# A diffusion block with adaptive layer norm: fewer and larger early loads, and the first rows of scale behind the transposes

## The chip, the cores and the metric

The kernel runs on one core of a Trainium2 chip. The core has a matrix engine (TensorE, PE in the profile, with PEld for its weight loads), a vector engine (VectorE, DVE), an activation engine (ScalarE, ACT), a general engine (GpSimd, POOL) and SyncE (SP), whose queue issues nearly all loads and stores. Sixteen DMA engines move the data between the chip's main memory (HBM) and the on-chip memory (SBUF); TensorE writes to accumulators in PSUM.

The metric is the time of one execution on the device, in microseconds (us); lower is better.

## The reference

B = 2 sequences of N = 256 tokens, width D = 1152, all tensors in bfloat16. Scale, shift and gate come from the vector c; the tokens are normalised, modulated, and go through one attention of a single head.

```python
mod = (_silu(c) @ w_mod).reshape(B, 6, 1, D)
shift_a, scale_a, gate_a, shift_m, scale_m, gate_m = [mod[:, i] for i in range(6)]
h = _layernorm(x, axis=-1) * (1 + scale_a) + shift_a
qkv = h @ wqkv
q, k, v = (qkv[..., :D].copy(), qkv[..., D:2 * D].copy(), qkv[..., 2 * D:].copy())
p = _softmax(jnp.einsum('bqd,bkd->bqk', q, k) * D ** (-0.5), axis=-1)
a = jnp.einsum('bqk,bkd->bqd', p, v) @ wo
return x + gate_a * a
```

Only the first three of the six parts of w_mod are used: shift (0), scale (1) and gate (2).

## The kernel before

**Tiles.** The 512 tokens are four tiles of 128 (t = 0 and 1 are sequence 0, t = 2 and 3 sequence 1). The width of 1152 is KT = 9 blocks of 128. The blocks fall into three parts of KA = 3: columns 0 to CA = 384, CA to CM = 768, and CM to D. w_mod is laid out with nine rows kk for each partition (line 49), so that a sum over c's width is a sum over the nine rows, and the kernel speaks of "rows" of scale and shift in this sense. K's weights (wK) have nine rows k, one for each block of the width of h.

**Loads.** Line 142 on defines `load_x` (a token tile, 288 KB), `load_mod` (some rows and columns of one part of w_mod) and `load_k` (rows and columns of K's weights); lines 151 to 174 issue them on SP's queue in this order: x tiles 1, 0 and 3; the first part of scale, as five loads of two rows (the last of one); K's row 0 in two pieces (3 blocks, then the 5 that are left of the first WE = 1024 columns), row 1, x tile 2, K's row 2; scale's second part in three loads of three rows; K's rows 3 to 5; scale's third part in three loads; K's rows 6 to 8; shift (wH) in five loads of two rows, the last of one; what is left of K's rows 0 to 2. The loads of Q's and V's weights, of the gate and of wo follow on the same queue. Eight completion semaphores are used in turn, so that a load on this queue is issued when the eighth load before it (the one of c counted) has landed; before, the first load that waits so is the fifth one of scale. c is loaded by ScalarE's queue.

**Opening on TensorE.** Twelve products of a constant tile (`fillers(12)`, line 185) come first, then two products that put the 1 of (1 + scale) into the accumulators psSA and psS0. `scale_A(kk)` (line 298) adds one row of the first part of scale: three products of 54 columns, into psS0 for block 0 and psSA for blocks 1 and 2. `turned` transposes the nine blocks of a centred token tile (xc) into two banks of PSUM (tp1a and tp1b, tp0a and tp0b), and `from_psum` copies them out to xnT, three blocks on VectorE and six on ScalarE. Lines 382 to 396 set the order: scale rows 0 and 1; tile 1's transposes and copies; rows 2 and 3; tile 0's transposes and copies; rows 4 to 8.

**After it.** `scaled(0, tok(0), psS0[:, 0:1])` on VectorE multiplies block 0 of sequence 0 with its finished scale, straight from psS0, and writes hTs; `k_part` (line 335) then starts to sum K in six accumulators (accs) and `early_half` a part of the next two blocks (psE). Tiles 3 and 2 follow in the same way. The second part of scale is summed in psM (rows 0 to 5, other work, then rows 6 to 8), the third in psL (all nine rows in one go), and the shift in psH by `shift_rows` (36 products, line 321). Then come Q, the scores, V, the attention and the output, all on TensorE, while VectorE works on the gate.

**Order.** The order of instructions on each engine is that of the program: each engine's calls are recorded by a helper (`_Rec`, line 78, which is why the profile gives L78 for nearly all of them) and chained by `pin` at the end. So the groups are told apart by the tiles that they write and read.

Of the kernel before, what the change touches and what calls it, by code (L numbers as in the profile page):

```python
# [16 lines left out]
def kernel(  # L17
# [11 lines left out]
    B, N, D = x.shape  # L29
    T = B * N  # L30
    KT = D // P
# [9 lines left out]
    WE = (NACC + NEARLY) * P  # L41
# [97 lines left out]
    wS = wmpool.tile([P, KT, D], BF16, tag="wS")  # L139
    wH = wmpool.tile([P, KT, D], BF16, tag="wH")  # L140

    def load_x(t):
        spq.dma_start(out=x_sb[:, t, :], in_=x_f[t * P : (t + 1) * P, :])

    def load_mod(tile_, which, k0, k1, c0, c1):
        spq.dma_start(out=tile_[:, k0:k1, c0:c1], in_=wmod_v[:, k0:k1, which, c0:c1])

    def load_k(k0, k1, c0=0, c1=D):
        spq.dma_start(out=wK[:, k0:k1, c0:c1], in_=wqkv_v[:, k0:k1, D + c0 : D + c1])

    PAIRS = ((0, 2), (2, 4), (4, 6), (6, 8), (8, 9))
    CA = KA * P
    load_x(1)
    load_x(0)
    load_x(3)
    for k0, k1 in PAIRS:
        load_mod(wS, 1, k0, k1, 0, CA)
    load_k(0, 1, 0, CA)
    load_k(0, 1, CA, WE)
    load_k(1, 2, 0, WE)  # L160
    load_x(2)
    load_k(2, 3, 0, WE)
    CM = KM * P
    for k0 in range(0, KT, 3):
        load_mod(wS, 1, k0, k0 + 3, CA, CM)
    for k in range(KA, KM):
        load_k(k, k + 1)
    for k0 in range(0, KT, 3):
        load_mod(wS, 1, k0, k0 + 3, CM, D)
    for k in range(KM, KT):  # L170
        load_k(k, k + 1)
    for k0, k1 in PAIRS:
        load_mod(wH, 0, k0, k1, 0, D)
    load_k(0, KA, WE, D)

# [28 lines left out]
    def sc_rhs(kk):  # L204
        return scT_rep[:, kk].rearrange("p r b -> p (r b)")
# [37 lines left out]
    def turned(tp, cols):  # L243
        for j, (t, k) in enumerate(cols):
            ten.transpose(tp[:, j, :], xc[:, t, k * P : (k + 1) * P], ident)

    def tiles_of(t, k0, k1):
        return [(t, k) for k in range(k0, k1)]

    def from_psum(eng, t, k0, k1, tp, j0=0):  # L250
        dst, srct = xnT[:, k0:k1, t * P : (t + 1) * P], tp[:, j0 : j0 + k1 - k0, :]
        if eng is vec:
            vec.tensor_copy(out=dst, in_=srct)
        else:
            sca.copy(out=dst, in_=srct)
# [42 lines left out]
    def scale_A(kk):  # L298
        for j in range(KA):
            ten.matmul(  # L300
                psS0 if j == 0 else psSA[:, j - 1, :], lhsT=wS[:, kk, j * P : (j + 1) * P], rhs=sc_rhs(kk),
                start=False, stop=(kk == KT - 1), skip_group_check=True,
            )
# [75 lines left out]
    def bank(name="tp", n=KT - KA, pool=psum, tag="mm"):  # L379
        return pool.tile([P, n, P], BF16, tag=tag, name=name)  # L380

    tp1a, tp1b, tp0a, tp0b = bank(n=KA), bank(), bank(n=KA), bank()
    for kk in range(2):
        scale_A(kk)
    turned(tp1a, tiles_of(1, 0, KA))
    turned(tp1b, tiles_of(1, KA, KT))
    from_psum(vec, 1, 0, KA, tp1a)
    from_psum(sca, 1, KA, KT, tp1b)
    for kk in range(2, 4):
        scale_A(kk)  # L390
    turned(tp0a, tiles_of(0, 0, KA))
    turned(tp0b, tiles_of(0, KA, KT))
    from_psum(vec, 0, 0, KA, tp0a)
    from_psum(sca, 0, KA, KT, tp0b)
    for kk in range(4, KT):
        scale_A(kk)
    act_var(0)

# [333 lines left out]
```

## Time and profile before

| what | value |
|---|---|
| time, median of 3 runs (lowest to highest) | 96.02 us (95.85 to 96.29) |
| the profiled execution: its own time, its span | 95.77 us, 94.0 us |
| TensorE's matmuls, of the whole span | 89.7 us (95%), 677 instructions |
| 12 fillers (junk_ps) | 1.11 to 6.41 us |
| first product on K (acc) | 8.86 us |
| loads moved by DMA engines, over the span | 21.31 MB, mean 227 GB/s |

The profile is of one execution. Its span runs from the first instruction of the program to the last; the execution's own time is 1.77 us longer. Times inside the profile are counted from the start of the span. A weight load (PEld) lies beside matmuls (PE) and precedes the product that uses it. Matmuls are pipelined: the times of single ones overlap, and the chain of waits gives each the time that it adds. "Landing" is when the last of a load's parts has told its semaphore, and the DMA view gives the time from issue to landing.

### The profile page before, as it was taken

What the parts mean: (1) busy time and instruction counts of PE and PEld (TensorE: products, weight loads), DVE (VectorE), ACT (ScalarE), POOL (GpSimd) and SP (SyncE); (2) the same over time, 40 slices, a digit from 0 to 9 for tenths busy, and PEclk for the clock granted to TensorE, in tenths of its full rate; (3) what the DMA queues carried; (4) which work ended last, traced back from release to release, by engine and by line L of the source; (5) the groups of instructions that cost most, each with busy time, mean ns of one, the idle gap of its engine ahead of it and who ended that gap; (6) DMA issues with size and microseconds to landing.
All of it is one profiled execution on the core that took longest, in us unless ns stands there. A gap on an engine that the chain in (4) does not pass through costs nothing.

```text
span 94.0 us, 1729 instructions
## 1 busy us (share of the span) xinstructions
PE 89.7 (95%) x677; PEld 54.4 (58%) x681; DVE 70.8 (75%) x137; ACT 33.3 (35%) x65; POOL 22.2 (24%) x28
## 2 busy tenths in 40 slices
PE   5998999999999999999999999999999999999980
PEld 1337998464454444444468666665678665666760
DVE  0496779154998999999997999982038487999870
ACT  5297867002845933223320474232226300000020
POOL 6720002800000000000000000009999970043000
PEclk9999999999999999999999999999999999999999
DMA  1999999999999999999999702200000000303131
GB/s 71 318 345 361 367 400 369 403 411 408 387 368 401 379 407 404 373 372 366 370 407 412 310 27 56 61 2 0 0 0 0 0 0 7 125 7 119 70 127 54
DMA packets 19015, 21.31 MB, mean 227 GB/s; under 512 B 2752, under 2 KB 13632, under 8 KB 19008
## 3 DMA queue, kind: packets, MB, share of 16 engines
q1 hardware_dynamic: 18592, 21.16, 62.5%
q10 hardware_dynamic: 416, 0.05, 0.4%
q8 instruction: 5, 0.08, 0.3%
q14 instruction: 2, 0.02, 0.0%
HBM read 19.76 MB, written 1.18 MB: 223 GB/s over the span
## 4 chain that ended last, share of the span: by engine, by line
PE 95%; DVE 1%; issue 0%; ACT 0%
PE ps L78 65%; PE acc L78 13%; PE junk_ps L78 6%; PE s_ps L78 4%; PE tp L78 2%; PE psE L78 1%; PE psH L78 1%; PE psL L78 1%; PE psM L78 1%; PE psSA L78 1%; PE psS L78 0%; DVE hTs L78 0%; PE spread_ps L78 0%; ACT o_sb L78 0%; DVE junk_rhs L78 0%
## 5 line engine op out<-in xcount | busy, mean ns | idle before, releaser
L78 POOL PARTITION_ALL_REDUCE gate_bc<-gacc x2 | 13.7, 6886 | 44.5 <-DVE gacc L78 44.5
L78 DVE SCALAR_TENSOR_TENSOR gacc<-wG,scT_f,gacc 128x1152 f32<-128x1152 bf16 x16 | 22.7, 1417 | 0.5
L78 PE MATMUL ps<-wqv,hT 128*128 128x384 bf16 x108 | 17.7, 326 | 0.0
L78 PE MATMUL ps<-hT,wqv 128*128 128x512 bf16 x80 | 17.6, 379 | 0.1
L78 PE MATMUL ps<-wO,attnT 128*128 128x384 bf16 (+1 forms) x108 | 17.0, 319 | 0.0
L78 PEld LDWEIGHTS <-attnT 128*128 128x128 bf16 x126 | 11.4, 98 | 6.3
L78 PEld LDWEIGHTS <-hT 128*128 128x128 bf16 x108 | 10.6, 98 | 6.9
L78 PEld LDWEIGHTS <-wK 128*128 128x128 bf16 x123 | 10.3, 97 | 6.7 <-issue 0.7
L78 PE MATMUL acc<-hTs,wK 128*128 128x128 bf16 (+2 forms) x88 | 13.4, 291 | 0.4 <-DVE hTs L78 0.3
L78 PEld LDWEIGHTS <-wqv 128*128 128x128 bf16 x81 | 7.9, 98 | 9.6
L78 ACT CAST qkT<-ps 128x512 bf16<-128x512 f32 x10 | 5.7, 584 | 10.8 <-PE ps L78 10.8
L78 DVE TENSOR_TENSOR ga<-ps,gate_bc 128x384 f32<-128x384 f32 (+1 forms) x12 | 6.5, 538 | 2.3 <-PE ps L78 2.3
L78 ACT CAST v_sb<-ps 128x384 bf16<-128x384 f32 x10 | 4.7, 475 | 9.8 <-PE ps L78 9.8
L78 DVE TENSOR_TENSOR o_sb<-ga,x_sb 128x384 bf16<-128x384 f32 (+1 forms) x12 | 6.8, 564 | 0.4
L78 ACT CAST o_sb<-ps 128x128 bf16<-128x128 f32 (+1 forms) x2 | 0.5, 238 | 17.0 <-PE ps L78 17.0
L78 DVE TENSOR_TENSOR xnT<-xnT,rstd_bc 128x512 bf16<-128x512 bf16 x9 | 5.5, 685 | 1.3 <-ACT rstd_bc L78 1.3
L78 PE MATMUL junk_ps<-junk_rhs 128*128 128x512 bf16 x12 | 5.3, 632 | 1.1 <-DVE junk_rhs L78 1.1
L78 DVE BATCH_NORM_STATS2 stats<-x_sb 128x6 f32<-128x384 bf16 x6 | 3.2, 554 | 2.5 <-DMA x_sb<-in_x_dram 2.5
L78 PE MATMUL ps<-hTs,wK 128*128 128x512 bf16 x20 | 4.8, 380 | 0.1
L78 DVE CAST attnT<-ps 128x512 bf16<-128x512 f32 (+1 forms) x6 | 3.5, 603 | 1.7 <-PE ps L78 1.7
L78 DVE CAST v_sb<-ps 128x384 bf16<-128x384 f32 x2 | 1.1, 557 | 4.6 <-PE ps L78 4.6
L78 DVE TENSOR_SCALAR hTs<-xnT,s1p 128x256 bf16<-128x256 bf16 (+1 forms) x20 | 4.3, 273 | 0.1
(82 smaller groups left out, 88.6 us busy)
## 6 DMA issues: line engine op xcount, KB each, us to landing
wqv<-in_wqkv_dram SPq DMA_DIRECT2D x5, 864.0 KB, 10.4
wG<-in_w_mod_dram SPq DMA_DIRECT2D x3, 864.0 KB, 9.4
wO<-in_wo_dram SPq DMA_DIRECT2D x3, 864.0 KB, 8.9
wH<-in_w_mod_dram SPq DMA_DIRECT2D x4, 576.0 KB, 8.2
wS<-in_w_mod_dram SPq DMA_DIRECT2D x6, 288.0 KB, 6.0
wK<-in_wqkv_dram SPq DMA_DIRECT2D x6, 288.0 KB, 6.3
x_sb<-in_x_dram SPq DMA_DIRECT2D x4, 288.0 KB, 3.3
wqv<-in_wqkv_dram SPq DMA_DIRECT2D x3, 288.0 KB, 8.5
```

Of the source, the lines that this page charges most:

```text
L78: r = fn(*a, **k)
```

## The change

In the loads, the three parts of scale are each loaded in two pieces, rows 0 to 4 and rows 5 to 8, instead of five, three and three pieces. The columns of K's row 0 come in one load instead of two. The shift comes in four loads of 3, 3, 2 and 1 rows instead of five. In the order on TensorE, tile 1's transposes come first, then scale rows 0 to 4, tile 0's transposes, and rows 5 to 8. The bytes that are loaded, and the order in which they are asked for, stay as they were, and so do all instructions on TensorE, VectorE, ScalarE and GpSimd, in number and shape; SP's queue has seven loads fewer, and the first load on it that waits for the landing of the eighth load before is now that of x tile 2.

```diff
-    PAIRS = ((0, 2), (2, 4), (4, 6), (6, 8), (8, 9))
+    PARTS = ((0, 5), (5, KT))
     CA = KA * P
     load_x(1)
     load_x(0)
     load_x(3)
-    for k0, k1 in PAIRS:
+    for k0, k1 in PARTS:
         load_mod(wS, 1, k0, k1, 0, CA)
-    load_k(0, 1, 0, CA)
-    load_k(0, 1, CA, WE)
+    load_k(0, 1, 0, WE)
     load_k(1, 2, 0, WE)
     load_x(2)
     load_k(2, 3, 0, WE)
     CM = KM * P
-    for k0 in range(0, KT, 3):
-        load_mod(wS, 1, k0, k0 + 3, CA, CM)
+    for k0, k1 in PARTS:
+        load_mod(wS, 1, k0, k1, CA, CM)
     for k in range(KA, KM):
         load_k(k, k + 1)
-    for k0 in range(0, KT, 3):
-        load_mod(wS, 1, k0, k0 + 3, CM, D)
+    for k0, k1 in PARTS:
+        load_mod(wS, 1, k0, k1, CM, D)
     for k in range(KM, KT):
         load_k(k, k + 1)
-    for k0, k1 in PAIRS:
+    for k0, k1 in ((0, 3), (3, 6), (6, 8), (8, KT)):
         load_mod(wH, 0, k0, k1, 0, D)
     load_k(0, KA, WE, D)
...
     tp1a, tp1b, tp0a, tp0b = bank(n=KA), bank(), bank(n=KA), bank()
-    for kk in range(2):
-        scale_A(kk)
     turned(tp1a, tiles_of(1, 0, KA))
     turned(tp1b, tiles_of(1, KA, KT))
     from_psum(vec, 1, 0, KA, tp1a)
     from_psum(sca, 1, KA, KT, tp1b)
-    for kk in range(2, 4):
+    for kk in range(5):
         scale_A(kk)
     turned(tp0a, tiles_of(0, 0, KA))
     turned(tp0b, tiles_of(0, KA, KT))
     from_psum(vec, 0, 0, KA, tp0a)
     from_psum(sca, 0, KA, KT, tp0b)
-    for kk in range(4, KT):
+    for kk in range(5, KT):
         scale_A(kk)
     act_var(0)
```

## The prediction

> **What bounds the kernel now.** I read the page's busy shares first, then what TensorE waited for, then the chain of waits over the whole span.
>
> ```profile
> span 94.0 us, 1729 instructions
> ...
> PE 89.7 (95%) x677; PEld 54.4 (58%) x681; DVE 70.8 (75%) x137; ACT 33.3 (35%) x65; POOL 22.2 (24%) x28
> ...
> DMA  1999999999999999999999702200000000303131
> ```
>
> ```profile
> PE junk_ps L78 <- DVE junk_rhs L78: 1.1, 1, 1.1
> PE acc L78 <- DVE hTs L78: 0.3, 1, 0.3
> ```
>
> TensorE is the bound. It starts its fillers at 1.1 us and waits once more in the whole execution, 0.3 us for the first scaled block (hTs). The DMA row has digit 9 from 2.4 us to about 52 us: the engines that move the loads never run dry, so a load lands when the bytes ahead of it are through. Next the chain of waits in order of time (start, duration, what):
>
> ```profile
> 1.11 5.30 PE junk_ps L78 x12
> 6.41 0.20 PE psSA L78
> ...
> 6.99 0.50 PE tp L78 x9
> ...
> 7.65 0.50 PE tp L78 x9
> ...
> 8.52 0.30 DVE hTs L78
> 8.82 0.04 issue
> 8.86 0.81 PE acc L78 x6
> ...
> 29.06 10.74 PE ps L78 x49
> ```
>
> All that the change moves on TensorE lies between the fillers' end (6.41) and 8.86, where K's accumulation starts. From there TensorE runs without a gap over 0.1 us to its last product at 91.3, so whatever arrives late at 8.86 comes late at the end, and no more can be gained than the one stall. The timeline shows who is ready when (start, duration, engine, what):
>
> ```profile
> 6.04 0.95 DVE L78 TENSOR_SCALAR xc<-x_sb,mv 128x1152 bf16<-128x1152 bf16 x2
> ...
> 6.58 0.30 PEld L78 LDWEIGHTS <-wS 128*128 128x128 bf16 x6
> ...
> 6.81 0.51 PEld L78 LDWEIGHTS <-xc 128*128 128x128 bf16 x9
> ...
> 7.93 0.49 PEld L78 LDWEIGHTS <-wS 128*128 128x128 bf16 x15
> ```
>
> The two rows of scale (6 weight loads of wS) now run while VectorE still centres token tile 1 (xc). Last, the five early scale loads, each in a narrow stretch of the queue's timeline and of the DMA view; the first and the last of them:
>
> ```profile
> 2.17 0.43 SPq L78 DMA_DIRECT2D wS<-in_w_mod_dram  x1
> wS<-in_w_mod_dram SPq DMA_DIRECT2D x1, 192.0 KB, 4.0
> ...
> 4.19 0.47 SPq L78 DMA_DIRECT2D wS<-in_w_mod_dram  x1
> wS<-in_w_mod_dram SPq DMA_DIRECT2D x1, 96.0 KB, 3.9
> ```
>
> Issue plus time to landing gives the landing: 2.17 + 4.0 = 6.2 (rows 0-1). The other stretches give 2.65 + 4.0 = 6.65 (2-3), 3.16 + 4.0 = 7.2 (4-5), 3.67 + 4.1 = 7.8 (6-7), and 4.19 + 3.9 = 8.1 (8). K's row 0 follows at 4.70 + 3.6 = 8.3 (its first 3 blocks) and 5.17 + 3.5 = 8.7 (the other 5), K's row 1 at 5.64 + 4.0 = 9.6.
>
> **The change, part by part.**
>
> *Seven loads fewer on SP's queue* (5 to 2, 2 to 1, 3 to 2 twice, 5 to 4). Bytes, their order and the 768-byte runs of scale stay. Each issue took 0.34 to 0.49 us of the queue, so the first scale part and K's row 0 are issued in three issues instead of seven, and what follows goes out some 1.9 us sooner (4 x 0.47). But the transfer engines are busy throughout (the windows from 5.5 to 8.5 show a DMA share of 1.02 to 1.14), so a load issued sooner stands longer in line. I cost it at nothing. Bounds: no loss, and a gain of at most 0.3 us, the stall of TensorE that is left.
>
> *Scale's first part in rows 0-4 and 5-8.* Rows 0-4 land between the old rows 2-3 (6.65) and 4-5 (7.2), half way, 6.9. Rows 5-8 land with the old row 8, at 8.1 at the latest; by rate, 864 KB (885 kB) at the 369 GB/s of the window 6.0 to 6.5 would take 2.4 us after the third x load's landing (1.71 + 3.5 = 5.2), so 7.6 at the soonest. Rows 5, 6 and 7, which had landed at 7.2 and 7.8, now wait for row 8's bytes.
>
> *Scale behind the transposes.* TensorE now goes to tile 1's transposes at once. xc of tile 1 is ready at 6.04 + 0.52 (the median of the four centrings) = 6.56; from such an end to the first product I take 0.05 (hTs ends 8.81, acc starts 8.86) plus 0.04 (weight load 9.69 to transpose 9.73), so 6.65: 0.07 us of idling where two rows of scale ran before.
> Up to about 6.8 TensorE is also slow. The twelve fillers take 5.30 us, 0.44 each, where twelve products of the same 512 columns take 2.75 us from 24.71 on, 0.22 each; the first two scale rows take 0.25 us (6.58 to 6.83), the next two 0.16 (7.33 to 7.49). In 6.65 to 6.82 half of the transposes' rate is lost, 0.08 us; with scale in that place 0.09 was lost, so this part cancels.
> In sequence: nine transposes 6.65 + 0.50 + 0.08 = 7.23; rows 0-4, 15 products at 0.026 (in the chain the 27 products of psL take 0.69), to 7.62, loaded since 6.9; nine transposes to 8.12; rows 5-8, 12 products, 0.31, to 8.43. Before, the last product's successor would have been due at 7.93 + 0.06 + 15 x 0.026 = 8.38. So **+0.06 us**, if rows 5-8 are there at 8.12. Against a landing of 8.1 that is a margin of zero, against 7.6 half a microsecond; a wait's restart costs about 0.05. I take +0.10, with 0 and +0.15 as this step's ends. What is late next is the first hTs on VectorE (8.52) and K's first product.
> Elsewhere: the copy of tile 0's transposes on VectorE moves from 7.85 to about 8.0 and ends at 8.36, before 8.6, when the first hTs comes due; ScalarE's first copy moves ahead and its second stays near 8.28, since transposes of tile 0 end 0.13 later but the copy ahead of it ends sooner. Both are covered.
>
> *K's row 0 in one load*, landed at 8.7 instead of 8.3 and 8.7. First use 8.86 (now 8.96): covered, by 0.2 us; every microsecond beyond costs one.
>
> *Scale's second and third parts, five and four rows.* Row 5 of the second part comes with rows 6-8 (issued 8.22, landed 8.22 + 5.2 = 13.4) instead of with 3-4 (7.79 + 4.8 = 12.6). Its product is due 15 products of 0.026 after 13.40, 13.8: 0.4 us of cover. Third part: landed 11.82 + 7.0 = 18.8, row 5 due 18.99 + 0.39 = 19.4: 0.6 us. No cost while they hold.
>
> *Shift in 3, 3, 2 and 1 rows.* Last row 18.84 + 8.8 = 27.6, due after 32 of the 36 products that start at 27.39 over 1.29 us, 28.5: covered by 0.9.
>
> **Sum.** 0.00 + 0.10 + 0 + 0 + 0 on the profiled execution: 95.77 (span 94.0 and 1.77 around it) becomes 95.87. That execution lies 0.25 under the median of the runs, 96.02, and the same 0.1 on the median gives **96.1 us**. About 0.5%, 0.48 us, is what a measurement of this kernel can tell from no change; its runs alone differ by 0.44.
>
> **Rivals.**
>
> *A slow transfer makes the larger load late (slower).* A load has landed when its last part has. The third-part scale load issued at 10.41 landed at 17.3 (6.9 us), 1.7 us after the last K load ahead of it (9.76 + 5.8 = 15.6), where the next ones come 0.8 apart: a slip of 0.9. It cost nothing there, as psL starts at 18.99. If one falls on rows 5-8 of the first part (8.1 + 0.9 = 9.0 against 8.12), TensorE stands 0.9 us: 96.0 + 0.9 + 0.1 = **97.0 us**; on the second part (cover 0.4), 96.6. It decides from a landing after 8.12 + 0.4. For it: four rows now hang on one landing. Against: row 8 hung on the same bytes before, with only 0.25 us of cover (8.1 against 8.33), and TensorE had no wait there. Chance 0.14.
>
> *Full speed comes at another moment.* The step from 0.44 to 0.22 us per 512 columns at about 6.8 belongs to no instruction that I can name; the change puts a short idle and other products just before it. If it came 1.7 us later, the 1.55 us of products up to 8.38 would be half done by then: +0.8, **96.9 us**; chance 0.10. If it came sooner, the fillers would shrink, but scale cannot end before 8.1 + 0.31, so at most 0.3 is gained against this execution, 95.77 - 0.3, which is 0.55 under the median: **95.5 us**; chance 0.09. The Trainium skill (TensorE: Matmul & The Clock Gate, Part 1: The HAM clock gate) says that half rate is the default, that sustained activity of a window of about 3.4 us lifts it, and that the window runs freely, so the moment shifts by run; the step at 6.8 agrees with half rate before it, and by that rule the change cannot choose its side.
>
> *Fewer, larger loads land sooner.* If each load dropped took its issue time of 0.47 with it, rows 5-8 would be there 3 x 0.47 = 1.4 us sooner, and all further loads too. Then only the 0.06 of the sequence counts, and TensorE's stall stays, as the last scale row is still computed at 8.43: **96.0 us**, no change. Chance 0.17. Against it are landings 0.5 us apart at a full DMA share. The Trainium skill (DMA: Bandwidth & Descriptors, Rules for kernel authors) says to coalesce small transfers into large ones, and puts full bandwidth at 1 MiB and more per DMA; here 192 KB loads pass at 369 GB/s, so the trace does not bear the gain out, and on this path it would buy nothing.
>
> **How the numbers follow.** My forecast (96.1) has 0.50. With the sooner loads (0.17) it is within 0.5%: 0.67, less 0.01 for an unlucky median on each side, 0.65. Slower: 0.14 + 0.10 + 0.01 = 0.25. Faster: 0.09 + 0.01 = 0.10. The likeliest case's own range is 95.8 to 96.4; to leave out no more than 2 in 10 I go down to 95.5, near the sooner full speed, and up to 96.7, which takes in a late second part and half of the two slower rivals.
>
> **What would show it.** After: fillers to 6.4, nine transposes from about 6.65, five scale rows at 7.2, nine transposes, four scale rows at 8.1 to 8.2, K's first product at 8.9 to 9.0. Scale's two first loads landed at 6.9 and 8.1 or sooner. A TensorE wait on wS or wK among its waits shows the first rival; 512-column products still 0.44 apart after 6.8, the second. Wrong would be a DMA share with holes before 50 us, a stall of over 0.4 us anywhere from 8.9 to 91, or landings over a microsecond sooner with an end that moves.

## The result and the profile after

The changed kernel takes 97.53 us (median of 15 runs, 96.50 to 100.1) where the kernel before took 96.20 in the same comparison (15 runs, 95.85 to 96.62). It is slower: ratio 1.009, 95% interval 1.0065 to 1.0115. This ratio leaves out five of the fifteen executions (98.32 to 100.1 us), in which TensorE was granted a mean clock of 0.965 to 0.983; they turn out to hold the same loss and a stretch of half speed behind it, and the profiled execution (99.52 us) is one of them.

The page of the kernel after, busy shares and the 40 slices:

```profile
span 97.8 us, 1726 instructions
...
PE 91.5 (94%) x681; PEld 55.3 (57%) x681; DVE 70.4 (72%) x137; ACT 33.6 (34%) x65; POOL 22.2 (23%) x28
...
PEclk9999579999999999999999999999999999999999
DMA  2989999999999999999999701210000000303131
```

Before, the DMA row had digit 9 from the second slice on. Now the third slice (4.9 to 7.3 us) has an 8, and in the fifth and sixth the clock (PEclk) is at 5 and 7 tenths. What TensorE waited for, in the kernel after (total, times, longest):

```profile
PE psS L78 <- DMA wS<-in_w_mod_dram: 1.8, 1, 1.8
PE junk_ps L78 <- DVE junk_rhs L78: 1.1, 1, 1.1
PE acc L78 <- DVE hTs L78: 0.3, 1, 0.3
PE tp L78 <- DVE xc L78: 0.2, 1, 0.2
```

The first row is new: 1.8 us for a load of scale, just behind tile 1's transposes. The chain of waits of the kernel after leads straight into that load (start, duration, what):

```profile
2.18 7.11 DMA wS<-in_w_mod_dram
9.29 0.05 issue
9.33 0.20 PE psS L78
...
9.89 0.54 PE tp L78 x9
...
11.03 0.30 DVE hTs L78
11.33 0.04 issue
11.38 1.44 PE acc L78 x6
```

K's first product runs at 11.38 instead of 8.86, and its six products take 1.44 us instead of 0.81. So of the 3.8 us by which this span is longer, 2.5 come before K's first product and 1.3 behind it. In two later executions with the same two loads of scale, in which the clock stayed up (e4 and e10 below), K's first product is only 0.8 us late, which is nearer to the ratio. The DMA view of the kernel after, in narrow stretches, for scale's two loads (issued at 2.18 and 2.65) and K's row 0 (issued at 3.22), with KB and time to landing:

```profile
wS<-in_w_mod_dram SPq DMA_DIRECT2D x1, 480.0 KB, 7.1
...
wS<-in_w_mod_dram SPq DMA_DIRECT2D x1, 384.0 KB, 7.7
...
wK<-in_wqkv_dram SPq DMA_DIRECT2D x1, 256.0 KB, 7.7
```

So rows 0 to 4 landed at 9.3, rows 5 to 8 at 10.35 and K's row at 10.9, where the prediction had 6.9, 8.1 and 8.7. The bytes ahead of them were the same. The windows show where the time went; first the kernel before, then after (stretch, length, busy time of PE, PEld, DVE, ACT, POOL, then PEclk, DMA share, GB/s):

```profile
5.00:6.00 1.00, 1.00 (x4) 0.22 (x2) 0.97 (x3) 0.97 (x3) 0.45 (x1) 1.00 1.03 332
6.00:7.00 1.00, 1.00 (x13) 0.55 (x13) 0.95 (x2) 0.89 (x2) 0.00 (x0) 1.00 1.10 369
```

```profile
5.00:6.00 1.00, 1.00 (x4) 0.22 (x2) 0.97 (x4) 1.00 (x2) 0.59 (x1) 1.00 0.79 199
6.00:7.00 1.00, 0.83 (x7) 0.32 (x7) 0.96 (x3) 0.97 (x3) 0.00 (x0) 1.00 0.99 253
```

Between 5 and 7 us the loads moved at 199 and 253 GB/s instead of 332 and 369: some 250 KB less. From 5 to 6 us the engines for transfers were not full (0.79), although scale's two loads and K's first rows had been issued by then; from 6 to 7 us they were (0.99), but moved fewer bytes than before.

### The profile page after: what moved, and what is told of

Its sections match the earlier page's. It is cut to its first block, busy times and chain, and to the rows that moved or that the text cites. A ratio compares the mean times of both kernels' runs of the same rounds, so it can differ in the third digit from the quotient of the medians.

```text
span 97.8 us, 1726 instructions
## 1 busy us (share of the span) xinstructions
PE 91.5 (94%) x681; PEld 55.3 (57%) x681; DVE 70.4 (72%) x137; ACT 33.6 (34%) x65; POOL 22.2 (23%) x28
## 4 chain that ended last, share of the span: by engine, by line
PE 87%; DMA 7%; SPq 1%; issue 0%; DVE 0%; ACT 0%
PE ps L78 63%; PE acc L78 13%; DMA wS<-in_w_mod_dram 7%; PE s_ps L78 4%; PE tp L78 2%; PE psE L78 2%; SPq L78 1%; PE psH L78 1%; PE psM L78 1%; PE psL L78 1%; PE psS L78 1%; PE psSA L78 1%; DVE hTs L78 0%; PE spread_ps L78 0%; ACT o_sb L78 0%
## 5 line engine op out<-in xcount | busy, mean ns | idle before, releaser
L78 PE MATMUL acc<-hTs,wK 128*128 128x128 bf16 (+2 forms) x90 | 14.2, 302 | 0.3 <-DVE hTs L78 0.3
L78 DVE COPY xnT<-tp 128x384 bf16<-128x384 bf16 (+1 forms) x6 | 1.8, 312 | 5.9 <-PE tp L78 5.9
```

The lines of the kernel that those rows point to most:

```text
L78: r = fn(*a, **k)
```

## The experiments

Four things were open at first: the order on TensorE, the loads of scale's first part, the other merged loads, and the clock. The table has what each profiled execution showed (landing = issue plus time to landing; all in us) and the comparison with the kernel before on the same chip; the chips differ between the groups of experiments, so ratios are compared and not times.

| kernel | scale's first load landed | scale's last load landed | K's first product | time, lowest to highest | ratio (95%) |
|---|---|---|---|---|---|
| before | 6.2 | 8.1 | 8.86 | 95.85 to 96.62 | |
| after | 9.3 | 10.35 | 11.38 | 96.50 to 100.1 | 1.009 (1.0065 to 1.0115) |
| e1 order alone | 6.2 | 8.1 | 8.85 | 96.00 to 97.27 | 1.0014 (0.998 to 1.0047) |
| e2 loads alone | 8.2 | 9.35 | 10.85 | 96.74 to 99.88 | none, 4 runs |
| e4 first part alone | 7.8 | 8.75 | 9.64 | 96.67 to 99.5 | 1.0099 (1.0057 to 1.0141) |
| e3 after, pairs in the first part | 6.4 | 9.1 | 9.75 | 96.65 to 97.29 | 1.0058 (1.0031 to 1.0084) |
| e5 after, threes | 7.5 | 9.1 | 9.82 | 96.54 to 96.91 | 1.0034 (1.000 to 1.0068) |
| e6 after, one load of nine | 8.7 | 8.7 | 10.43 | 97.36 to 100.87 | 1.0108 (1.0006 to 1.0211) |
| e13 order, and 2, 3, 4 rows | 7.0 | 8.9 | 9.71 | 96.44 to 98.19 | 1.0068 (1.0039 to 1.0096) |
| e11 order, and parts 2 and 3 | 6.4 | 8.3 | 8.95 | 96.00 to 97.47 | 1.0037 (1.0001 to 1.0072) |
| e12 order, K's row 0, shift | 6.1 | 8.5 | 9.14 | 96.23 to 97.28 | 1.0042 (1.0019 to 1.0065) |
| e9 after, seven fillers | 7.9 | 9.5 | 10.46 | 97.35 to 97.78 | 1.0129 (1.0089 to 1.017) |
| e7 after, rows 0 to 4 by blocks | 6.2 | 8.7 | 9.56 | 97.34 | none, 1 run |
| e8 after, K's rows 0 and 1 ahead, pairs | 7.9 | 9.8 | 10.46 | 97.83 | none, 1 run |
| e10 after, later loads held back | 7.8 | 8.75 | 9.64 | 97.29 | none, 1 run |
| after once more | 8.9 | 9.85 | 11.57 | 100.37 | none, 1 run |

**The order alone (e1)**: before, with lines 382 to 396 as after.

```diff
-    for kk in range(2):
-        scale_A(kk)
     turned(tp1a, tiles_of(1, 0, KA))
...
-    for kk in range(2, 4):
+    for kk in range(5):
         scale_A(kk)
...
-    for kk in range(4, KT):
+    for kk in range(5, KT):
         scale_A(kk)
```

> Loads as before, only the order on TensorE as after. Theory A (the five-row load of scale's first part is handed out slowly, some transfer engines get their share late): no wait on wS over 0.2 us, rows 0-4 found loaded, K's first product at 8.9 to 9.0, ratio 1.000 to 1.002. Rival C (the new order itself costs, since rows 0 and 1 no longer run ahead of the transposes): a good part of the loss, ratio 1.005 or more, and an idle stretch before the transposes instead of one at wS.

The ratio can't be told from 1. TensorE in the timeline of e1 (the idle time before it and what ended it in brackets):

```profile
6.64 0.68 PE L78 MATMUL tp<-ident,xc 128*128 128x128 bf16 x9 [1.02 <-DVE xc L78]
...
8.85 0.81 PE L78 MATMUL acc<-hTs,wK 128*128 128x256 bf16 x6 [0.33 <-DVE hTs L78]
```

In this execution full speed came at 4.3 us, so the fillers ended a microsecond sooner and TensorE stood idle until xc; the transposes still start at 6.64 and K's first product is at 8.85. The sequence that the prediction worked out holds, and rival C falls.

**The loads alone (e2)**: after, with the order on TensorE of before.

> Loads as after, the order on TensorE as before. Theory A: scale's first load still lands at 8 to 9.3 us, TensorE now waits for it before the transposes, with nothing to do from 6.4 on, so as slow as after or slower: ratio 1.008 to 1.03, K's first product at 10.5 or later. Rival C: ratio 1.000 to 1.002.

Theory A held: 97.1 us of span, a wait of 1.8 us for wS, now ahead of the transposes. There is no ratio, since three of the four executions had the lowered clock. So the loss comes with the loads, whatever the order on TensorE; whether the new order makes it smaller, four executions don't tell.

**The first part alone (e4)**: e1 with this one edit.

```diff
-    for k0, k1 in PAIRS:
+    for k0, k1 in ((0, 5), (5, KT)):
         load_mod(wS, 1, k0, k1, 0, CA)
```

> Before with scale's first part alone in two loads of five and four rows, and the order on TensorE of after; all other loads as before. Theory A: first load lands at 8 to 9.3, TensorE waits 1 to 2 us for it, ratio 1.006 to 1.03, as after. Rival D: lands near 6.9, ratio under 1.003.

The whole loss is back: 1.0099 against 1.0014 for e1, whose interval ends (1.0047) below where that of e4 begins (1.0057). The chain of waits of e4 leads into the same load as in the kernel after:

```profile
2.17 5.57 DMA wS<-in_w_mod_dram
7.74 0.05 issue
7.79 0.20 PE psS L78
```

Two expectations were missed. The first load landed at 7.8, 0.2 under what was expected, and no wait of 1 to 2 us for it is seen: in this execution tile 1 was centred 0.4 us late, TensorE stood 1.2 us for xc, and the load landed just as the transposes ended.

**The first part back in pairs, the rest as after (e3).**

> After, with scale's first part alone back in pairs (landings of before: 6.2, 6.7, 7.2, 7.8, 8.1). Theory A: landings back at those of before within 0.3 us, no wait on wS over 0.2 us, K's first product near 8.9, ratio 0.999 to 1.003. Rival D (the loss comes from the loads behind, which are larger or issued sooner and share the engines): scale's first part still lands at 8.5 or later and the ratio stays over 1.006.

Half held: the first row pair landed at 6.4, but row 8 only at 4.21 + 4.9 = 9.1, and 1.0058 is over what Theory A allowed. The trace also keeps the moments at which the 16 shares of a load told its semaphore: 15 of row 8's shares were in by 8.4, so much of its delay is one late share. But the interval lies above 1, so other merged loads seem to cost too, which e11 and e12 take apart below.

**Three rows, and nine (e5, e6)**: after, with the first part in three loads of three rows, or in one.

> After, with scale's first part in three loads of three rows (24 runs of 768 bytes for each of 16 transfer engines, where five rows are 40 and pairs 16). Theory A (what counts is how many runs one load gives each engine): first load lands at 6.5 to 7.2, between pairs and fives, DMA share from 5 to 6 us over 0.9, ratio between that of pairs (1.006 with the other loads as in after) and of after (1.009). Rival T (a threshold between 24 and 40): landings as by the bytes, rows 0-2 at 6.5 and the last at 8.1.

> After, with scale's first part in one load of nine rows (72 runs for each engine). Theory A: handed out slower still, lands at 10 us or later, DMA share under 0.8 for over 2 us from 5 us on, TensorE waits 2.5 us or more for it, time 98 us or more. Rival S (a load's end is late only because of the rows behind it, and the transfer itself goes at full rate): lands where the old row 8 did, 8.1 to 8.5.

Threes can't be told from pairs (1.0034 and 1.0058, with intervals that overlap), so their ratio doesn't lie between pairs and fives as Theory A had it; their landings say little, since in this execution one share of the third x load was late (6.7) and held the first rows back. Nine refute Theory A as it stood: the 72 runs for each engine landed at 8.7, no later than the last of five and four rows anywhere, with a DMA share of 0.93 to 1.05 between 5 and 7 us. That is 0.6 behind row 8 of before, no more than the 0.8 or more of the first load with half the bytes: the delay does not grow in proportion to size. The times are still bad (97.36 to 100.87), because row 0 then waits for row 8: TensorE stood 1.4 us. So a larger load can cost in two ways, by its own delay and by making the first row as late as the last one.

**Runs or bytes (e7, e8).** e7 is after with rows 0 to 4 in three loads of one block of columns each (160 KB, 640 runs of 256 bytes). e8 is after with pairs in the first part, and K's rows 0 and 1 (512 KB, 256 runs of 2048 bytes) in one load ahead of them.

```diff
-    for k0, k1 in PARTS:
-        load_mod(wS, 1, k0, k1, 0, CA)
+    for j in range(KA):
+        load_mod(wS, 1, 0, 5, j * P, (j + 1) * P)
+    load_mod(wS, 1, 5, KT, 0, CA)
```

> After, with rows 0-4 of scale's first part in three loads of one block of columns each: 160 KB, less than a pair's 192 KB, but 640 runs of 256 bytes, as many as the five-row load has. Theory A (runs, not bytes): SP's issues behind are held up as in after (0.6 us or more each), DMA share falls under 0.9 and under 250 GB/s, the third lands at 9 or later. Rival B (bytes of one load): they land as pairs do, about 6.1, 6.5 and 6.9.

> K's rows 0 and 1 in one load of 512 KB directly behind the three x loads, where the five-row load of 480 KB stands in after; scale's first part in pairs behind it. It has 256 runs of 2048 bytes, 16 for each engine. Theory A: lands at 6.6 to 7.0 (5.3 + 512 KB at 369 GB/s = 6.7), no dip in the DMA share before 7 us. Rival B (bytes): lands at 8 to 9.3 as the five-row load did, with a share of about 0.8. The time says little here, as scale comes 1.4 us later: 97 to 98 us.

The DMA view of e7, for loads issued at 2.18, 2.65, 3.22 and 3.89:

```profile
wS<-in_w_mod_dram SPq DMA_DIRECT2D x1, 160.0 KB, 4.0
...
wS<-in_w_mod_dram SPq DMA_DIRECT2D x1, 160.0 KB, 4.0
...
wS<-in_w_mod_dram SPq DMA_DIRECT2D x1, 160.0 KB, 4.1
...
wS<-in_w_mod_dram SPq DMA_DIRECT2D x1, 384.0 KB, 4.8
```

Landings of 6.2, 6.65 and 7.3: 1920 small runs are through 0.4 us behind the 6.9 of their bytes, and half a microsecond or more ahead of every single load of the same 480 KB. These loads also ask for five rows of a partition before the next partition, as the five-row load does and pairs do not, so that order does not seem to be what delays it. The time is no better for it (97.34 us), since rows 5 to 8, still in one load, landed at 8.7 and TensorE waited 0.4 us for them. In e8 the 512 KB with few runs landed at 2.18 + 5.2 = 7.4 instead of 6.7, and the same hole stands in its window from 5 to 6 us:

```profile
5.00:6.00 1.00, 1.00 (x4) 0.23 (x2) 0.96 (x3) 0.97 (x3) 0.45 (x1) 1.00 0.82 232
```

With one execution of each, this points to the size of one load (Rival B) rather than the number of its runs; but 7.4 lies between the two expectations of e8, and the one load of 864 KB in e6 had no hole between 5 and 6 us (340 GB/s), so size alone is not the whole account. The issues behind the small-run loads were held up, as Theory A has it (1.50 us for the fourth load of e7), but these landings came when they did all the same.

**The loads behind, held back (e10)**: after, with K's row 0, and so everything behind it, issued when the last filler has ended.

```diff
-    load_k(0, 1, 0, WE)
+    held = load_k(0, 1, 0, WE)
...
     fillers(12)
+    tc.add_manual_dep(held.ins, pe_seq[-1].ins.name, SYNC_SCHED, reason="hold")
```

> After, with K's row 0 and so all loads behind it issued only when TensorE's fillers have ended (5.4 to 6.4 us), so that only x and scale's first part are in line before. Theory D (loads issued ahead spoil the transfer of those in front): scale's first part lands by the bytes, 6.9 and 8.1, DMA share over 0.95 from 5 to 6 us. Theory L (a large load is slow by itself): 7.7 or later and 8.7 or later, DMA share 0.75 to 0.85 between 5 and 6. K's row 0 lands at 8.5 to 9.5 either way, time 97 or more.

Theory L: with nothing behind them, scale's loads (issued at 2.18 and 2.65) still landed at 7.8 and 8.75, as in e4, and the window of e10 from 5 to 6 us has the hole. So the delay is there without loads behind; whether those add to it in executions with landings of 9.3, one execution doesn't tell.

```profile
5.00:6.00 1.00, 1.00 (x4) 0.22 (x2) 0.93 (x4) 0.97 (x3) 0.31 (x1) 1.00 0.81 227
```

**A small load ahead (e13)**: e1 with the first part in loads of two, three and four rows.

> Order of after, loads of before, but scale's first part in three loads of two, three and four rows. Theory Q (only the first large load behind x starts badly; a small one ahead heals it): landings by the bytes, 6.2, 7.0 and 8.1, ratio 1.000 to 1.003. Theory L (each load is late by its own size): 6.2, 7.2 to 7.5, 8.5 or later, ratio 1.003 to 1.007.

Theory L by the ratio, 1.0068, and the last landing, 8.9. The landings themselves, 7.0, 7.75 and 8.9, say less: a share of the third x load was late, and with it the first of these loads, of which 15 shares of 16 were in by 6.2.

**The other merged loads (e11, e12).** e11 is e1 with scale's second and third parts in five and four rows; e12 is e1 with K's row 0 in one load and the shift in four.

> The kernel with the order of after and all loads of before (ratio 1.0014), with scale's second and third parts in five and four rows. Reads where the rest of the loss with pairs (1.0058) comes from. Theory E (large loads cost wherever they stand early): ratio 1.003 to 1.006, the loads in front of or behind the second part land 0.3 us or more later than with threes. Rival F (only the first part matters, the rest covers itself): 1.000 to 1.002.

> Order of after, loads of before, but K's row 0 in one load and the shift in four. Theory E (large loads cost only where they stand at the head of the stream, ahead of a waiting TensorE): ratio 1.000 to 1.003, as the order alone (1.0014), K's row 0 landed by 8.9, K's first product at 8.8 to 9.0. Rival K (the merged K row is what pairs do not win back): ratio 1.004 to 1.007, a wait on wK or hTs at 9 us or later.

e11 is unclear: its ratio of 1.0037 can't be told from that of e1, and its lowest time is that of e1. e12 is slower than before, 1.0042, in the range of Rival K, but its interval overlaps that of e1 as well, so the ratio alone does not show a price of K's merged row. The weight loads in the timeline of e12:

```profile
8.53 0.14 PEld L78 LDWEIGHTS <-wS 128*128 128x128 bf16 x3 [0.19 <-DMA wS<-in_w_mod_dram]
9.14 0.77 PEld L78 LDWEIGHTS <-wK 128*128 128x128 bf16 x8 [0.47 <-DMA wK<-in_wqkv_dram]
```

K's row landed at 4.70 + 4.4 = 9.1 instead of 8.7, and the first weights for K waited for it. In this execution row 8 was late as well (8.5), so hTs was ready only at 9.06. With hTs on time (8.8) the product would still have waited for the row until 9.1: the cover of 0.2 that I had named was gone, which costs up to 0.3 (9.14 against 8.85 in e1). How much of it is due to the merge is not shown, since the late share of row 8 (15 of 16 were in by 7.9) went ahead of K's row.

**The clock (e9, and after once more).** e9 is after with `fillers(7)` between tile 1's transposes and the five scale rows.

> After, with seven filler products (1.5 us at 0.22) between tile 1's transposes and the five scale rows, where TensorE waits for wS. Theory H (part of what after loses is the clock, halved for a stretch because TensorE stood idle): no execution with a mean clock under 0.99, the highest times fall from 100.1 to under 98, median 96.8 to 97.2; the lowest stay near 96.5. Rival W (the wait alone; the clock has its own causes): the same spread as after, 96.5 to 100, with clocks of 0.965 to 0.983 among them.

None of the six executions of e9 had a clock under 0.99, and the times are 97.35 to 97.78 (ratio 1.0129, 1.0089 to 1.017): the executions over 98 are gone. At the rate of after, 5 in 15, six without one would come by chance about once in eleven. Gone, too, are those near 96.5, since the fillers end at 8.9 even where the load has landed at 7.9. The median, 97.51, is that of after: nothing is won.

> The changed kernel once more, to see how far the landings of scale's first part differ by execution. Theory L: the first load lands anywhere from 7.5 to 9.3, the second 1.0 to 1.2 later, K's first product 1.2 us after the second landing, and the span is that product's start plus 85.4 (as in the other kernels at full clock). Rival: 9.3 and 10.3 again, the same by the microsecond.

The loads landed at 8.9 and 9.85, and K's first product came at 11.57, 1.7 behind the second landing and not 1.2, as the clock was down already from 8.4 on, before the first load had landed. The span of 98.6 is 87.0 us over that product; in the profiles at full clock this is 85.1 to 85.9, in after 86.4. What goes before a lowered clock, in windows of after, of after once more, and of e6, where it stayed up (columns as above):

```profile
6.80:10.20 3.40, 1.54 (x33) 1.38 (x33) 0.85 (x3) 1.40 (x3) 0.00 (x0) 1.00 1.04 368
10.20:13.60 3.40, 3.10 (x30) 2.40 (x28) 2.03 (x8) 3.12 (x5) 0.19 (x1) 0.50 1.08 384
```

```profile
5.02:8.43 3.41, 1.61 (x15) 0.76 (x13) 2.28 (x6) 3.07 (x5) 0.46 (x1) 1.00 0.93 276
8.43:11.84 3.41, 2.62 (x38) 2.46 (x39) 0.96 (x6) 1.19 (x3) 0.00 (x0) 0.50 1.06 387
11.84:15.25 3.41, 3.41 (x22) 2.67 (x21) 2.05 (x9) 2.56 (x5) 0.19 (x1) 0.50 1.07 394
```

```profile
4.68:8.09 3.41, 1.78 (x16) 0.81 (x13) 2.65 (x7) 3.09 (x5) 0.59 (x1) 1.00 0.98 317
8.09:11.50 3.41, 2.44 (x48) 2.21 (x49) 1.77 (x8) 1.79 (x3) 0.00 (x0) 1.00 1.05 387
```

The first stretch of each begins where the clock was first granted in full, and each lasts 3.4 us. Where TensorE was busy for 1.54 or 1.61 of it (and 1.61 in e2), the next stretch ran at 0.50; at 1.78 in e6 it did not, nor in the other twelve profiles, where it was busier still. In after once more a half-speed stretch with 2.62 us of work was followed by a second one; in after, with 3.10, full speed came back. Behind K's first product, the half-speed stretches cost 1.0 us in after and 1.6 in after once more (86.4 and 87.0 against some 85.4 at full clock). Executions with a lowered clock occurred in after (5 of 15, and once more), e2 (3 of 4), e4 (3 of 10), e6 (2 of 4) and e13 (1 of 7), and in none of before, e1, e3, e5, e9, e11 and e12.

## Why the prediction was wrong

**The step that failed** is this: "Rows 0-4 land between the old rows 2-3 (6.65) and 4-5 (7.2), half way, 6.9. Rows 5-8 land with the old row 8, at 8.1 at the latest". It put bytes in a line and let a load land when its last byte's turn came, however the line was cut. In all six profiles with the first part in five and four rows (after twice, e2, e4, e9, e10) the first load landed at 7.8 to 9.3 and the second at 8.75 to 10.35. The words "at the latest" were wrong: the loads directly behind x in the profile before had 96 to 192 KB, and nothing in it showed a larger one at that place. The margin that I named, zero, was that of rows 5 to 8; the longest wait, 1.8 us in after, came on rows 0 to 4, "loaded since 6.9" and due at 7.23, and hid the late landing of the others.

The traces show how the step fails, since they keep the moment of each of a load's 16 shares. In before, the shares of rows 4 and 5 came from 6.5 to 7.2. In the six profiles with 480 KB in one load, its first share came at 6.2 to 6.5, its eighth at 6.6 to 7.6 and its last at 7.75 to 9.3 (in after 6.4, 7.3 and 9.3). So there is not one line of bytes: some shares are through about when the bytes say, others 1.3 to 2.9 us behind them, and the landing is that of the last.

**The order on TensorE**, +0.10 taken, 0 to +0.15 as ends: borne out, as far as the runs can tell. e1 shows -0.01 on K's first product and 1.0014 (0.13 us) on the time, but its interval is about 0.3 us wide to either side. **The merged K row**, called covered by 0.2: the cover is gone when the row lands at 9.1, which costs up to 0.3 in e12; the ratio does not tell it from the order alone. **Scale's second and third parts and the shift**, no cost: not refuted for scale, as e11 can't be told from e1; the shift was not tried by itself. **Seven loads fewer**, nothing gained: so it was; the issues went out sooner, but the larger loads landed later.

**The rivals.** The first one had the right end (97.0 at 0.14, a late load from 8.12 on, price one for one), but on rows 5 to 8, as a chance slip of one transfer, and with the argument against it that row 8 hung on the same bytes before; a late landing came in every profile with these loads. The second had TensorE at half speed for longer, but because full speed would come late; what the runs show is a fall back to half after full speed had come, behind a stretch in which TensorE mostly waited. So it is less a rival of the first than a consequence. The sooner landings of the third did not occur in any profile. The Trainium skill (DMA: Bandwidth & Descriptors, Rules for kernel authors) recommends loads of 1 MiB and more for bandwidth. No load here is that large, and at this place larger ones brought no more: between 5 and 6 us 332 GB/s with loads of 192 KB (before), 139 to 300 with 480 KB (six profiles), 340 with 864 KB (e6).

**What stays open** is why a large load starts slowly behind the x tiles. The cut of the first part decides (e4 against e1); single executions speak against the number of runs (e7) and against the loads behind (e10) as the cause; and one load of 864 KB (e6) is delayed less than its size would have it. Later in the stream, between 8 and 10 us, the loads of the kernel after move at 396 GB/s. Which engines carry the late shares, and what they lack, these runs do not tell. Late shares also occur with small loads in single executions (x in e5 and e13, row 8 in e12).

## What to carry to other kernels

A load's landing is not its place in a line of bytes: the consumer waits for the slowest share of the whole load, so cut the loads that stand between the start and the first dense work to what one step of the consumer needs, and merge only where there is cover to spare. Before a merge, read the cover of each piece's first use, not that of the last byte. And price a wait on TensorE twice where it may leave the engine busy for less than half of a 3.4 us stretch: the wait itself, and the half-speed stretch behind it (1.0 to 1.6 us here).

## What the runs showed of the hardware

There are two things that I had not expected. In these profiles the clock of TensorE fell to half for a stretch of 3.4 us after one of the same length in which it was busy for 45 to 47% of the time (three profiles), and not after 52% (e6); it need not be idle throughout. The Trainium skill (TensorE: Matmul & The Clock Gate, Part 1) gives the 3.4 us window, which these records show, and speaks of an idle window before the fall; here one that was busy for 45 to 47% was enough.

The moment of full speed wanders from execution to execution: 4.1 to 7.1 us after the start in these profiles. It moves the end of the fillers by about a microsecond, but hardly K's first product (8.85 with full speed at 4.3, 8.86 at 6.8), since xc and the loads then take over the wait.
